# Building an expert's list of tokens: three tiles of tokens in one TensorE product in place of two

## The chip, the core and the metric

The kernel runs on one core of a Trainium2 chip. A core has a matrix engine (TensorE, PE in the profile; PEld is its weight load), VectorE (DVE), ScalarE (ACT), GpSimd (POOL) and SyncE (SP), each with an instruction queue of its own, and 16 DMA engines. The metric is the device time of one execution in microseconds. Before the change it is 648.73 us, the median of three runs (648.26 to 650.05).

## The reference, cut to what matters

Sliding-window attention (batch 8, 8 heads, 576 positions, 64 per head) makes 4608 tokens of 512 values. Then a mixture of 8 experts: all (token, expert) pairs are sorted by their logits, and in that order a token goes to an expert that has room (at most 576 tokens each). Each expert applies two matrices with a ReLU between.

```python
x = attn_out.transpose(0, 2, 1, 3).reshape(B * S, H * D)
logits = x @ w_gate
order = np.argsort(-logits.flatten())
for idx in order:                       # greedy, with capacity
    tok, e = idx // E, idx % E
    if assigned[tok] >= 0 or counts[e] >= cap:
        continue
    assigned[tok] = e; counts[e] += 1
for e in range(E):
    mask = assigned == e
    out[mask] = np.maximum(x[mask] @ w1[e], 0.0) @ w2[e]
```

## The kernel before, in words

The first part, up to about 147 us, is the attention; it also writes the token rows `xs` to DRAM and keeps the gate logits of all tokens in SBUF, 36 tiles of 128 tokens (`NJ` is 36). Then `Routing` settles one expert at a time, in eight rounds `p` = 0 to 7, and `Experts` computes each expert's two layers. From here on "list p" is the list of round p. Round 0 stands alone, since no expert is known before it. The later rounds are recorded between the matrix products of the expert before.

The order of the instructions on every engine is written by a small planner (`Streams`): generators yield a planned duration (`self.busy(...)` for an engine, `self.dve(...)` for VectorE), and the planner resumes whichever is due. Each engine then runs its instructions strictly in that order, so an instruction that has to wait holds back all that stands behind it.

A round finds by search the threshold of the next full expert (lines 530 to 620), and then makes the list of its 576 tokens, in `steps`:

- Lines 655 to 672: a running count gives each chosen token its place 0 to 575 in the list. `sb` holds the place's quotient by 32 (0 to 17) and remainder (0 to 31), for each lane and tile of tokens.
- Line 683: `A` (128 lanes x 18 x 36 tiles, bf16) is 1 where the quotient equals a row number; the 36 tiles lie innermost. Line 687 (693 in round 0) makes `B` (32 x 36) in the same way from the remainder.
- Line 685 (ScalarE) writes `A` times the lane number into `R`, and line 691 (VectorE) writes `A` times the number of the tile's first token into `R`. `R` is the stationary operand: for each product 128 columns, of which the first 72 are used.
- Line 697: 18 products, each for two tiles of tokens. The stationary operand is `R` of the two tiles, the moving operand is `B` of the two, 32 x 2 columns: runs of two neighbours (4 bytes), one run every 36 elements (72 bytes). All add up in one PSUM area `il`.
- Line 701 copies `il` to `ils`. Line 706: small products with the constant `s5` add lane and tile parts and both tiles, and lay the list out as 128 x 5. Line 711 makes the integers `idx`, with which line 964 (GpSimd) gathers the tokens' rows `xg`.

In round 0 lines 691 and 693 run in two halves of 18 tiles, and the products of a half follow it. After line 706 of round 0 come 28 products that only keep TensorE running (line 475). The rows gathered are transposed at line 888 and go into the first layer (line 1127; line 1006 in the last two experts). Lines 1160 and 1168 are the second layer. Line 1095 (ScalarE) and line 1100 (VectorE) empty the first layer's sums.

Of the kernel before, what the change touches and what calls it, by code (L numbers as in the profile page):

```python
# [11 lines left out]
BF = mybir.dt.bfloat16  # L12
HF = mybir.dt.float16
I32 = mybir.dt.int32
AF = mybir.ActivationFunctionType
OP = mybir.AluOpType
# [12 lines left out]


def attention(ctx, tc, c, q, k, v, vt, gate, xs, L, choices, setup, counters):

    nc = tc.nc
# [169 lines left out]
    load_qk(0, 2, 4, nc.scalar)  # L203
    nc.sync.dma_start(wgbd, wg)
    counters()
    load_vt(0, 0, 4)
    load_vt(0, 4, NB)
# [143 lines left out]
NJ = NT // 128  # L351
# [9 lines left out]
class Routing:  # L361


    def __init__(self, ctx, tc, c, V):
        self.tc, self.nc, self.c, self.V = tc, tc.nc, c, V
        nc = tc.nc
        rt = ctx.enter_context(tc.tile_pool(name="rt", bufs=1))
        self.rt, self.ctx = rt, ctx

        def t(name, shape, dt=FT):  # L370
            x = rt.tile(shape, dt, name=name)
            setattr(self, name, x)
            return x

        for name in ("eid", "un", "m", "best"):
            t(name, [128, NJ])
        for name in ("oh", "w", "one"):
            t(name, [128, NJ, E], BF)
        t("G0", [128, NJ, ND], BF)
        t("cw", [128, E])  # L380
        t("dg", [128, ND], I32)
        t("sh", [128, NR], I32)
        t("v5", [72, 2, 4, 5], I32)
        t("lane", [128, 1])
        t("rows", [128, 1], U32)
        self.setup = self.constants(t)
        self.idx, self.eint = {}, {}

    def counters(self):
        iota = self.nc.gpsimd.iota  # L390
        iota(self.cw, pattern=[[-1, E]], base=E, channel_multiplier=0, allow_small_or_imprecise_dtypes=True)
        iota(self.dg, pattern=[[1, ND]], base=1, channel_multiplier=0)
        iota(self.sh, pattern=[[-4, NR]], base=28, channel_multiplier=0)
        iota(self.v5, pattern=[[1, 2], [2, 4], [8, 5]], base=0, channel_multiplier=-1)
        iota(self.v5[:, :, 2:4, 4], pattern=[[1, 2], [2, 2]], base=32, channel_multiplier=-1)
        iota(self.rows, pattern=[[0, 1]], base=0, channel_multiplier=1)
        iota(self.lane, pattern=[[0, 1]], base=0, channel_multiplier=1, allow_small_or_imprecise_dtypes=True)

    def constants(self, t):

        nc, jp = self.nc, self.c["jp"]
        cw, dg, lane = self.cw, self.dg, self.lane
        cw9 = t("cw9", [128, E])
        yield nc.vector.tensor_scalar(cw9, cw, -9.0, None, op0=OP.add)
        ones = t("ones", [128, 128], BF)
        yield nc.vector.memset(ones, 1.0)
        tri = t("tri", [128, 128], BF)

        yield nc.vector.tensor_scalar(tri, jp, 0.0, -1.0, op0=OP.is_le, op1=OP.mult)
        dgf = t("dgf", [128, ND])  # L410
        yield nc.vector.tensor_copy(dgf, dg)
        tab = t("tab", [128, NR, ND], I32)
        yield nc.vector.tensor_tensor(tab, dg[:, None, :].to_broadcast([128, NR, ND]),
                                      self.sh[:, :, None].to_broadcast([128, NR, ND]), OP.logical_shift_left)
        yield nc.vector.tensor_scalar(tab[:, 0, 0:7], tab[:, 0, 0:7], -1, None, op0=OP.bitwise_xor)
        yield nc.vector.tensor_scalar(tab[:, 0, 7:15], tab[:, 0, 7:15], -2 ** 31, None, op0=OP.bitwise_xor)

        for name, n in (("r32", 32), ("r18", 18)):
            yield nc.gpsimd.iota(t(name, [128, n, NJ], BF), pattern=[[1, n], [0, NJ]], base=0, channel_multiplier=0,
                                 allow_small_or_imprecise_dtypes=True)  # L420
        yield nc.gpsimd.iota(t("row", [128, 1, NJ], BF), pattern=[[0, 1], [128, NJ]], base=0, channel_multiplier=0,
                             allow_small_or_imprecise_dtypes=True)

        diag = t("diag", [128, 4])
        gt = t("gt", [32, 5])
        yield nc.vector.tensor_scalar(gt, jp[0:32, 0:33:8], 0.0, None, op0=OP.is_le)
        for q in range(4):
            yield nc.vector.tensor_tensor(diag[32 * q:32 * q + 32], gt[:, 0:4], gt[:, 1:5], OP.subtract)
        self.sq = [t(f"sq{i}", [128, 32]) for i in range(2)]
        self.pq = [t(f"pq{i}", [128, 32]) for i in range(2)]  # L430
        for x in self.sq + self.pq:
            yield nc.vector.memset(x, 0.0)

        s5 = t("s5", [72, 2, 4, 5], BF)
        w5 = t("w5", [72, 2, 4, 5])
        yield nc.vector.tensor_scalar(w5, self.v5, 0.0, None, op0=OP.is_equal)
        yield nc.vector.scalar_tensor_tensor(s5, self.v5, -36.0, w5, op0=OP.is_equal, op1=OP.add)

        t("st", [128, 5, E])
        self.left = self.st[:, 4]  # L440
        yield nc.vector.memset(self.left, -float(CAP))
        yield nc.vector.memset(t("all8", [128, E]), 1.0)
# [39 lines left out]
    def start(self):  # L482
        self.wk = self.ctx.enter_context(self.tc.tile_pool(name="rw", bufs=2))

        self.R = self.wk.tile([128, NJ // 2, 128], BF, name="R", bufs=1)
        self.nc.scalar.activation(self.R[:, :, 72:], self.r32[:, 0:28].rearrange("p a j -> p (a j)")
                                  .rearrange("p (q w) -> p q w", w=56), AF.Copy, scale=0.0)
        self.ps = self.ctx.enter_context(self.tc.tile_pool(name="rp", bufs=1, space=PSUM))

    def dve(self, dt):  # L490
# [3 lines left out]
    def steps(self, p):  # L494

        nc, wk, V = self.nc, self.wk, self.V
        m, best, one = self.m, self.best, self.one
        slack = SLACK[p]
        tile_ = wk.tile
        X = tile_([128, 2, NJ], BF, name="X")  # L500
        code = tile_([128, 1], FT, name="code")
        if p < E - 1:
# [17 lines left out]
            base = tile_([128, 1], I32, name="base")  # L520
            rest = []
            for r in range(NR):
# [14 lines left out]
                else:  # L537
# [9 lines left out]
                    for j in range(0, NJ, 4):  # L547
                        w = one4[:, j // 4] if own else one[:, j:j + 4]
                        nc.tensor.matmul(c4, w.rearrange("p k e -> p (k e)"),
                                         G[:, j:j + 4].rearrange("p j d -> p (j d)"),  # L550
                                         start=(j == 0), stop=(j == NJ - 4))
# [44 lines left out]
                else:  # L596
# [9 lines left out]
                    if r + 1 < NR:  # L606
                        nc.vector.scalar_tensor_tensor(thr2, self.tab[:, r + 1], d[:, 0:1],
                                                       base[:, 0:1].to_broadcast([128, ND]),
                                                       op0=OP.bitwise_xor, op1=OP.bitwise_xor)
                    base = b2  # L610
# [20 lines left out]
            q = tile_([128, NJ], FT, name="q", bufs=1)  # L631
# [13 lines left out]
        else:  # L645
# [19 lines left out]
                                       op0=OP.add, op1=OP.mult)  # L665
# [8 lines left out]
        B_ = tile_([128, 32, NJ], BF, name="B", bufs=1)  # L674
        R_ = self.R
        A_ = tile_([128, 18, NJ], BF, name="A", bufs=1)
        il = self.room(128, 64)
        Rw = R_[:, :, 0:72].rearrange("p q (k a h) -> p k a q h", k=2, h=2)

        def pairs(x):  # L680
            return x.rearrange("p a (q h) -> p a q h", h=2)

        nc.vector.tensor_tensor(A_, self.r18, sb[:, 0, None, :].to_broadcast([128, 18, NJ]), OP.is_equal)
        yield self.dve(410)
        nc.scalar.activation(Rw[:, 0], pairs(A_), AF.Copy, scale=self.lane)
        if p:
            nc.vector.tensor_tensor(B_, self.r32, sb[:, 1, None, :].to_broadcast([128, 32, NJ]), OP.is_equal)
            yield self.dve(670)
        for j0, j1 in ((0, NJ),) if p else ((0, 18), (18, 36)):
            n = j1 - j0  # L690
            nc.vector.tensor_tensor(Rw[:, 1, :, j0 // 2:j1 // 2], pairs(A_[:, :, j0:j1]), pairs(self.row[:, :, j0:j1].to_broadcast([128, 18, n])), OP.mult)
            if not p:
                nc.vector.tensor_tensor(B_[:, :, j0:j1], self.r32[:, :, j0:j1],
                                        sb[:, 1, None, j0:j1].to_broadcast([128, 32, n]), OP.is_equal)
            yield self.dve(600) + slack + (500 if p else 0)
            for j in range(j0, j1, 2):
                nc.tensor.matmul(il, R_[:, j // 2], B_[:, :, j:j + 2], start=(j == 0), stop=(j == NJ - 2))
            yield self.busy(n * 29)
        yield self.dve(200) + slack
        ils = tile_([72, 32, 2], BF, name="ils")  # L700
        nc.vector.tensor_copy(ils.rearrange("p a h -> p (a h)"), il[0:72])
        yield self.dve(300)
        ip = self.room(128, 5, not p)
        for g in range(4):
            for h in range(2):
                nc.tensor.matmul(ip[32 * g:32 * g + 32], ils[:, :, h], self.s5[:, h, g], start=(h == 0), stop=(h == 1))
        if p == 0:
            self.warm(28)
        yield self.busy(100) + 200 + slack
# [4 lines left out]
        if p < E - 1:  # L714
            if not p:
# [12 lines left out]
                                           op0=OP.is_gt, op1=OP.mult)  # L728
# [573 lines left out]
```

## Time and profile before

| | |
|---|---|
| median of three runs | 648.73 us |
| profiled execution | 649.96 us, span 648.3 us |
| TensorE busy | 610.8 us (94%) |
| VectorE busy | 472.0 us (73%) |
| ScalarE busy | 342.5 us (53%) |
| GpSimd busy | 223.3 us (34%) |

The span is the time from the first to the last instruction in the trace; the rest of the execution lies around it. Busy times of different engines overlap. A matmul's duration in the trace holds the time until its result is written, so products in a row start closer to each other than one lasts: the distance is read from a row that sums up several (last end less one duration, over the number less one).

### The profile page before, as it was taken

How to read it: one execution, taken by the hardware profiler on the slowest of the kernel's cores; microseconds unless marked ns; L12 is line 12 of the kernel's file. 1: busy time of each engine (PE TensorE's matmuls, PEld its weight loads, DVE VectorE, ACT ScalarE, POOL GpSimd, SP SyncE). 2: the span in 40 equal slices, each digit the busy share in tenths (PEclk: the TensorE clock that was granted, in tenths of full speed). 3: DMA queues.
4: the chain of work that ended last, by engine and by line, in shares of the span. 5: the costliest groups of instructions: out<-in, count | busy, mean ns of one | idle time of the engine just before them, and what ended most of it. 6: DMA issues, size and time to landing. Idle time of an engine off the chain costs nothing. (4 is left out here: it accounts for less than half of the span.)

```text
span 648.3 us, 17083 instructions
## 1 busy us (share of the span) xinstructions
PE 610.8 (94%) x6423; PEld 527.8 (81%) x6423; DVE 472.0 (73%) x2127; ACT 342.5 (53%) x598; POOL 223.3 (34%) x235
## 2 busy tenths in 40 slices
PE   7899999995599999999999999999999999899995
PEld 6787887784489779978987998898789879778984
DVE  6887887787787768876877786888678875674610
ACT  2477676671255177255546537264544557766710
POOL 5455655450241062133306115131521515223211
PEclk9999999996599999999999999999999999999998
DMA  8997968991476197679659579867938638977721
GB/s 320 373 383 268 351 232 341 365 343 53 148 220 131 38 312 192 124 259 220 150 164 254 154 145 289 190 144 242 198 132 197 206 102 219 266 174 185 156 58 40
DMA packets 40338, 135.16 MB, mean 208 GB/s; under 512 B 5176, under 2 KB 5304, under 8 KB 40256
## 3 DMA queue, kind: packets, MB, share of 16 engines
q0 software_dynamic: 15568, 54.03, 36.9%
q1 hardware_dynamic: 24400, 79.52, 33.9%
q8 instruction: 51, 0.84, 0.5%
q10 hardware_dynamic: 288, 0.52, 0.3%
q14 instruction: 31, 0.25, 0.1%
HBM read 82.15 MB, written 18.87 MB: 156 GB/s over the span
## 5 line engine op out<-in xcount | busy, mean ns | idle before, releaser
L1150 POOL DMA_INDIRECT out<-ot,idx x40 | 41.6, 1041 | 195.4 <-ACT ot L1141 42.2
L1168 PE MATMUL o<-wl,hh 128*128 128x512 f32 x256 | 101.5, 396 | 2.4 <-DMA wl<-st 2.4
L1168 PE MATMUL o<-wh,hh 128*128 128x512 f32 x256 | 102.4, 400 | 0.1
L1168 PE MATMUL o<-wh,hl 128*128 128x512 f32 x256 | 101.4, 396 | 0.0
L144 POOL TENSOR_TENSOR st<-st,mx 128x512 f32<-128x512 f32 x72 | 73.4, 1039 | 66.8 <-DVE mx L137 60.6
L851 ACT ACTIVATE wh<-st 128x1024 fp32r<-128x1024 f32 x72 | 75.7, 1053 | 8.5 <-DMA st<-w 4.7
L1095 ACT ACTIVATE hh<-h 128x256 fp32r<-128x256 f32 (+1 forms) x96 | 39.0, 407 | 75.5 <-PE h L1127 74.8
L862 POOL DMA_DIRECT2D wl<-st x63 | 58.3, 1140 | 56.0 <-ACT wl L860 40.3
L964 POOL DMA_INDIRECT xg<-xs,idx x40 | 42.8, 1070 | 91.9 <-DVE eq L718 66.5
L1127 PE MATMUL h<-xh,wl 128*128 128x320 f32 (+1 forms) x384 | 70.8, 300 | 0.0
L137 DVE CUSTOM_DVE_ANT_0 st<-Sp,mask 128x128 f32<-128x128 f32 x288 | 67.2, 283 | 4.8 <-PE Sp L128 4.1
L1127 PE MATMUL h<-xh,wh 128*128 128x320 f32 (+1 forms) x384 | 69.5, 300 | 0.7 <-ACT xh L954 0.7
L1127 PE MATMUL h<-xl,wh 128*128 128x320 f32 (+1 forms) x384 | 69.6, 299 | 0.3 <-DVE xl L958 0.3
L860 ACT ACTIVATE wl<-wh 128x1024 fp32r<-128x1024 f32 x63 | 66.5, 1056 | 0.7
L1168 PEld LDWEIGHTS o<-wl,hh 128*128 128x128 f32 x256 | 48.1, 188 | 12.1 <-DMA wl<-st 3.2
L1127 PEld LDWEIGHTS h<-xh,wh 128*128 128x128 f32 x384 | 56.8, 189 | 1.4 <-ACT xh L954 0.8
L1127 PEld LDWEIGHTS h<-xh,wl 128*128 128x128 f32 x384 | 57.2, 189 | 0.3
L1127 PEld LDWEIGHTS h<-xl,wh 128*128 128x128 f32 x384 | 56.8, 189 | 0.5 <-DVE xl L958 0.5
L1168 PEld LDWEIGHTS o<-wh,hh 128*128 128x128 f32 x256 | 48.2, 188 | 9.8 <-DVE ot L1148 0.5
L1168 PEld LDWEIGHTS o<-wh,hl 128*128 128x128 f32 x256 | 48.1, 188 | 9.3
L1141 ACT ACTIVATE ot<-o 128x512 f32<-128x512 f32 x32 | 19.1, 596 | 65.9 <-PE o L1168 58.8
L152 ACT ACTIVATE pt<-Tp 128x512 f32<-128x512 f32 x72 | 39.8, 594 | 21.0 <-PE Tp L150 19.8
(227 smaller groups left out, 1282.0 us busy)
## 6 DMA issues: line engine op xcount, KB each, us to landing
wl<-st POOLq DMA_DIRECT2D x63, 512.0 KB
st<-w SPq DMA_DIRECT2D x60, 512.0 KB
V<-v SPq DMA_DIRECT2D x16, 584.0 KB
xs<-x SPq DMA_DIRECT2D x36, 256.0 KB
VT<-vt SPq DMA_DIRECT2D x8, 640.0 KB
VT<-vt SPq DMA_DIRECT2D x8, 512.0 KB
Q<-q SPq DMA_DIRECT2D x6, 640.0 KB
K<-k SPq DMA_DIRECT2D x6, 640.0 KB
```

What stands on the lines that cost most here:

```text
L137: nc.vector.tensor_tensor_reduce(st[:, h, :], Sp[h % 2][:, h // 2], mk, scale=-0.125, scalar=3.0e38, op0=OP.add, op1=OP.min, accum_out=mx[ ...
L144: nc.gpsimd.tensor_tensor(st, st, mx[:, :, None].to_broadcast([128, 4, 128]), OP.subtract)
L152: nc.scalar.activation(pt, Tp, AF.Exp, scale=-1.0)
L851: nc.scalar.activation(hi, x, AF.Copy)
L860: nc.scalar.activation(lo, hi.bitcast(FT), AF.Copy, scale=-1.0)
L862: nc.gpsimd.dma_start(lo.bitcast(FT), x, accum_op=OP.add)
L964: nc.gpsimd.indirect_dma_start(out=g[0:n, a], out_offset=None, in_=self.xs, in_offset=IndirectOffsetOnAxis(ap=idx[0:n, a:a + 1], axis=0))
L1095: nc.scalar.activation(hh[:, f, c0:c1], h, AF.Relu)
L1127: nc.tensor.matmul(h, wv[:, cc, 128 * (f % 2):128 * (f % 2) + 128], xt[:, cc, c0:c1], start=(k == 0), stop=(k == 11))
L1141: nc.scalar.activation(ot, o, AF.Copy)
L1150: nc.gpsimd.indirect_dma_start(out=self.out, out_offset=IndirectOffsetOnAxis(ap=idx[0:m, a:a + 1], axis=0), in_=ot[0:m], in_offset=None)
L1168: nc.tensor.matmul(o, ht[:, f, 128 * a:128 * a + 128], wt[:, 512 * (f % 2):512 * (f % 2) + 512], start=(f == 0 and k == 0), stop=(f == NF ...
```

## The change

Three tiles of tokens go into one product: 12 products a list with 96 moving columns each, where 18 with 64 were. In `R` 108 of the 128 columns are used, and the rows of one tile lie next to each other (18 columns for each of the three tiles, for the lane part, and then the same for the tile part); before, the two tiles alternated. Lines 685 and 691 so write runs of 54 neighbours and read `A` across its 36 tiles, one element every 72 bytes. `s5` is built for three tiles, and line 706 becomes 12 products. The planned duration of the list's products falls from 29 to 20 ns for each tile.

```diff
-        t("v5", [72, 2, 4, 5], I32)
+        t("v5", [108, 3, 4, 5], I32)
...
-        iota(self.v5, pattern=[[1, 2], [2, 4], [8, 5]], base=0, channel_multiplier=-1)
-        iota(self.v5[:, :, 2:4, 4], pattern=[[1, 2], [2, 2]], base=32, channel_multiplier=-1)
+        iota(self.v5, pattern=[[18, 3], [1, 4], [4, 5]], base=0, channel_multiplier=-1)
+        iota(self.v5[:, :, 2:4, 4], pattern=[[18, 3], [1, 2]], base=16, channel_multiplier=-1)
...
-        s5 = t("s5", [72, 2, 4, 5], BF)
-        w5 = t("w5", [72, 2, 4, 5])
+        s5 = t("s5", [108, 3, 4, 5], BF)
+        w5 = t("w5", [108, 3, 4, 5])
...
-        self.R = self.wk.tile([128, NJ // 2, 128], BF, name="R", bufs=1)
-        self.nc.scalar.activation(self.R[:, :, 72:], self.r32[:, 0:28].rearrange("p a j -> p (a j)")
-                                  .rearrange("p (q w) -> p q w", w=56), AF.Copy, scale=0.0)
+        self.R = self.wk.tile([128, NJ // 3, 128], BF, name="R", bufs=1)
+        self.nc.scalar.activation(self.R[:, :, 108:], self.r32.rearrange("p a j -> p (a j)")[:, 0:20 * NJ // 3]
+                                  .rearrange("p (q w) -> p q w", w=20), AF.Copy, scale=0.0)
...
-        il = self.room(128, 64)
-        Rw = R_[:, :, 0:72].rearrange("p q (k a h) -> p k a q h", k=2, h=2)
-        def pairs(x):
-            return x.rearrange("p a (q h) -> p a q h", h=2)
+        il = self.room(128, 96)
+        Rw = R_[:, :, 0:108].rearrange("p q (k h a) -> p k q h a", k=2, h=3)
+        def threes(x):
+            return x.rearrange("p a (q h) -> p q h a", h=3)
...
-        nc.scalar.activation(Rw[:, 0], pairs(A_), AF.Copy, scale=self.lane)
+        nc.scalar.activation(Rw[:, 0], threes(A_), AF.Copy, scale=self.lane)
...
-            nc.vector.tensor_tensor(Rw[:, 1, :, j0 // 2:j1 // 2], pairs(A_[:, :, j0:j1]), pairs(self.row[:, :, j0:j1].to_broadcast([128, 18, n])), OP.mult)
+            nc.vector.tensor_tensor(Rw[:, 1, j0 // 3:j1 // 3], threes(A_[:, :, j0:j1]), threes(self.row[:, :, j0:j1].to_broadcast([128, 18, n])), OP.mult)
...
-            for j in range(j0, j1, 2):
-                nc.tensor.matmul(il, R_[:, j // 2], B_[:, :, j:j + 2], start=(j == 0), stop=(j == NJ - 2))
-            yield self.busy(n * 29)
+            for j in range(j0, j1, 3):
+                nc.tensor.matmul(il, R_[:, j // 3], B_[:, :, j:j + 3], start=(j == 0), stop=(j == NJ - 3))
+            yield self.busy(n * 20)
...
-        ils = tile_([72, 32, 2], BF, name="ils")
-        nc.vector.tensor_copy(ils.rearrange("p a h -> p (a h)"), il[0:72])
+        ils = tile_([108, 32, 3], BF, name="ils")
+        nc.vector.tensor_copy(ils.rearrange("p a h -> p (a h)"), il[0:108])
...
-            for h in range(2):
-                nc.tensor.matmul(ip[32 * g:32 * g + 32], ils[:, :, h], self.s5[:, h, g], start=(h == 0), stop=(h == 1))
+            for h in range(3):
+                nc.tensor.matmul(ip[32 * g:32 * g + 32], ils[:, :, h], self.s5[:, h, g], start=(h == 0), stop=(h == 2))
```

Although a planned duration changes, the order of the instructions stays almost as it was. On VectorE, GpSimd and SyncE nothing moves; on ScalarE one weight copy moves past one neighbour in the last expert; on TensorE two products move. The next two pieces are VectorE at list 6, before and after. Line 691 stands between the instructions of line 1100, and line 683, which it reads, stands two places ahead.

```order
L683 TENSOR_TENSOR A<-r_466,sb 128x648
L687 TENSOR_TENSOR B<-r_394,sb 128x1152
L1100 SCALAR_TENSOR_TENSOR hl<-h,hh 128x256
L691 TENSOR_TENSOR R<-A,row 128x18x18x2
L1100 SCALAR_TENSOR_TENSOR hl<-h,hh 128x256
L1100 SCALAR_TENSOR_TENSOR hh<-h,hh 128x64
L701 CAST ils<-rps 72x64
```

After the change, at the same place (the columns at the end are the pattern of what is written):

```order
L683 TENSOR_TENSOR A<-r_466,sb 128x648
L687 TENSOR_TENSOR B<-r_394,sb 128x1152
L1100 SCALAR_TENSOR_TENSOR hl<-h,hh 128x256
L691 TENSOR_TENSOR R<-A,row 128x12x54
L1100 SCALAR_TENSOR_TENSOR hl<-h,hh 128x256
L1100 SCALAR_TENSOR_TENSOR hh<-h,hh 128x64
L701 CAST ils<-rps 108x96
```

Nothing moved; line 691 writes 12 runs of 54 in place of 18 x 18 runs of 2, and line 701 copies 96 columns. The one place where TensorE's order differs is behind list 7, before and after: line 888 transposes the last rows of expert 7, and line 706 follows.

```order
L1168 MATMUL o<-wh,hh 128x512
L1168 MATMUL o<-wl,hh 128x512
L888 MATMUL tp<-identr,xg 128x64 x4
L1168 MATMUL o<-wh,hl 128x512
L706 LDWEIGHTS ils
L706 MATMUL rps<-s_808,ils 32x5
```

After the change:

```order
L1168 MATMUL o<-wh,hl 128x512
L1168 MATMUL o<-wh,hh 128x512
L888 MATMUL tp<-identr,xg 128x64 x4
L1168 MATMUL o<-wl,hh 128x512
L706 LDWEIGHTS ils
L706 MATMUL rps<-s_808,ils 32x5
```

The transposes and line 706 stand behind two more products of the second layer than before.

## Rows read from the trace of the kernel before

**Rows 1.** Stretches: busy us of each engine, granted clock, DMA share, GB/s.

```profile
200.00:540.00 340.00, 339.61 (x2470) 296.86 (x2469) 260.87 (x1040) 174.55 (x272) 103.66 (x105) 1.00 0.70 183
170.00:173.00 3.00, 1.10 (x18) 1.07 (x18) 2.25 (x8) 0.86 (x1) 0.00 (x0) 0.50 0.72 203
```

**Rows 2.** Groups of instructions: busy us, mean ns of one, idle before.

```profile
L549 PE MATMUL rps<-G,one 128*128 128x60 bf16 x360 | 17.1, 191 | 0.0
L697 PE MATMUL rps<-B,R 128*128 128x64 bf16 x144 | 9.9, 239 | 2.7 <-ACT R L685 2.5 <-DVE R L691 0.2
L685 ACT ACTIVATE R<-A,lane 128x648 bf16<-128x648 bf16 x8 | 7.1, 887 | 27.9 <-DVE A L683 27.9
L691 DVE TENSOR_TENSOR R<-A,row 128x648 bf16<-128x648 bf16 x7 | 5.2, 740 | 0.0
L731 DVE TENSOR_REDUCE c<-oh 128x8 bf16<-128x288 bf16 x7 | 4.7, 669 | 0.2
L458 DVE TENSOR_REDUCE best<-w 128x36 f32<-128x288 bf16 x6 | 2.7, 451 | 0.2
L1168 PE MATMUL o<-wl,hh 128*128 128x512 f32 x256 | 101.5, 396 | 2.4 <-DMA wl<-st 2.4
```

**Rows 3.** Timeline, one search product group: start us, length us, engine, line.

```profile
239.58 0.43 PE L549 MATMUL rps<-G,one 128*128 128x60 bf16 x9
```

**Rows 4.** Timeline of lists 1 to 7: line 691 and the products behind.

```profile
227.19 0.73 DVE L691 TENSOR_TENSOR R<-A,row 128x648 bf16<-128x648 bf16 x1
228.37 1.24 PE L697 MATMUL rps<-B,R 128*128 128x64 bf16 x18
...
281.11 0.73 DVE L691 TENSOR_TENSOR R<-A,row 128x648 bf16<-128x648 bf16 x1
282.52 1.24 PE L697 MATMUL rps<-B,R 128*128 128x64 bf16 x18
...
337.31 0.75 DVE L691 TENSOR_TENSOR R<-A,row 128x648 bf16<-128x648 bf16 x1
338.36 1.24 PE L697 MATMUL rps<-B,R 128*128 128x64 bf16 x18
...
391.44 0.75 DVE L691 TENSOR_TENSOR R<-A,row 128x648 bf16<-128x648 bf16 x1
392.36 1.24 PE L697 MATMUL rps<-B,R 128*128 128x64 bf16 x18
...
447.64 0.73 DVE L691 TENSOR_TENSOR R<-A,row 128x648 bf16<-128x648 bf16 x1
448.51 1.24 PE L697 MATMUL rps<-B,R 128*128 128x64 bf16 x18 [0.23 <-DVE R L691]
...
502.69 0.74 DVE L691 TENSOR_TENSOR R<-A,row 128x648 bf16<-128x648 bf16 x1
503.58 1.24 PE L697 MATMUL rps<-B,R 128*128 128x64 bf16 x18
...
522.98 0.75 DVE L691 TENSOR_TENSOR R<-A,row 128x648 bf16<-128x648 bf16 x1
524.26 1.24 PE L697 MATMUL rps<-B,R 128*128 128x64 bf16 x18
```

**Rows 5.** Timeline of list 0 and of the transposes that read its rows.

```profile
170.99 0.44 DVE L691 TENSOR_TENSOR R<-A,row 128x324 bf16<-128x324 bf16 x1
171.90 0.45 DVE L693 TENSOR_TENSOR B<-r,sb 128x576 bf16<-128x576 bf16 x1
171.90 1.24 PE L697 MATMUL rps<-B,R 128*128 128x64 bf16 x18 [2.52 <-ACT R L685]
...
179.36 0.40 PEld L888 LDWEIGHTS tp<-identr,xg 128*128 128x128 f32 x4 [0.79 <-DMA xg<-xs,idx]
```

**Rows 6.** Timeline, line 706 of list 1 and the next product.

```profile
230.29 0.23 PE L706 MATMUL rps<-s,ils 72*32 72x5 bf16 x8
230.45 0.50 PE L1168 MATMUL o<-wl,hh 128*128 128x512 f32 x1
```

More of the change, by code (lines that the diff above doesn't have):

```diff
@@ L432, in constants @@
             yield nc.vector.memset(x, 0.0)
-        s5 = t("s5", [72, 2, 4, 5], BF)
-        w5 = t("w5", [72, 2, 4, 5])
+        s5 = t("s5", [108, 3, 4, 5], BF)
+        w5 = t("w5", [108, 3, 4, 5])
         yield nc.vector.tensor_scalar(w5, self.v5, 0.0, None, op0=OP.is_equal)
-        yield nc.vector.scalar_tensor_tensor(s5, self.v5, -36.0, w5, op0=OP.is_equal, op1=OP.add)
+        yield nc.vector.scalar_tensor_tensor(s5, self.v5, -54.0, w5, op0=OP.is_equal, op1=OP.add)
         t("st", [128, 5, E])
```

## The prediction, made before the result was known

> **What bounds the kernel now.** I read the stretches first, by stage; then the groups of the lines that the change touches; then the timeline around each list. In the stretches the reader is to see that TensorE is busy 339.61 of the 340 us from 200 to 540 us, at a granted clock of 1.00, the upper level of 2.4 GHz [rows 1]. All of lists 1 to 7 lie there. A microsecond of TensorE's work that goes in this stretch, or a microsecond that TensorE has to wait, so moves the end by the same amount. List 0 stands by itself: in 170 to 173 us TensorE is busy 1.10 of 3 us at a granted clock of 0.50, the lower level of 1.2 GHz, and VectorE 2.25 [rows 1]. There the chain VectorE, list, gather, transposes sets the time: the transposes at 179.36 us wait for the DMA of the gathered rows [rows 5].
>
> The groups show what the list's instructions cost [rows 2], and the timeline shows how little time lies between the end of line 691 and the first product that needs it [rows 4]. At list 5 the products already wait for line 691: it ends at 447.64 + 0.73 = 448.37 us and they start at 448.51, so the hand-over takes 0.14 us. For each list the room is the products' start, less the end of line 691, less 0.14:
>
> - list 1: 228.37 - 227.92 - 0.14 = 0.31
> - list 2: 282.52 - 281.84 - 0.14 = 0.54
> - list 3: 338.36 - 338.06 - 0.14 = 0.16
> - list 4: 392.36 - 392.19 - 0.14 = 0.03
> - list 5: 0
> - list 6: 503.58 - 503.43 - 0.14 = 0.01
> - list 7: 524.26 - 523.73 - 0.14 = 0.39
>
> **The list's products.** Eighteen products end 1.24 us after the first starts, and one lasts 0.239 [rows 2, 4]: (1.24 - 0.24) / 17 = 0.0588 us from one to the next. The search's products, with as wide a stationary operand and 60 columns that lie side by side, follow each other after (0.43 - 0.19) / 8 = 0.030 us [rows 2, 3]. So the weight load is not what holds the list's products back: it is the moving operand `B`, in runs of two every 72 bytes. How runs of three do, no row shows. From below, the pace of columns side by side would be 96 / 60 x 0.030 = 0.048; a run that costs what it costs now gives 0.0588 (32 runs, as before); a column that costs what it costs now gives 96 / 64 x 0.0588 = 0.088. I take 0.072, between the last two, because the two rows that there are leave open whether the run or the column is what is paid. Then lists 1 to 7 take 7 x 12 x 0.072 = 6.05 us where they took 7 x 18 x 0.0588 = 7.41: -1.36. The ends are 4.03 (-3.38) and 7.39 (0).
>
> **Line 706.** Eight products hold TensorE from 230.29 to 230.45 us, 20 ns each, though all eight are over 0.23 us after the first starts [rows 6]: they overlap, so from below four more cost nothing. By the row they cost 0.08 a list, which I take: +0.56 over seven lists.
>
> **Line 691, the term that decides.** Now it takes 0.740 us for 648 elements, and 0.44 for 324 in list 0 [rows 2, 5]: 0.93 ns an element and a fixed 0.14. The change makes what it writes one run of 54 and what it reads one element every 72 bytes. The nearest row of a stepped bf16 read on VectorE is line 731, 288 elements in steps of 16 bytes: 669 ns. Line 458 reads as many side by side in 451 [rows 2]. Without the fixed part that is (0.669 - 0.14) / 288 = 1.84 ns an element stepped, and 1.08 side by side. So the new line 691 takes 0.14 + 648 x 1.84 = 1.33 us, 0.59 more. From below: 0.14 + 648 x 1.08 = 0.84, 0.10 more, if the step costs nothing. From above: if the step is paid twice (1.84 + 0.76), 1.82, 1.08 more. I take 1.33, the row that reads the same type in steps.
>
> The Trainium skill weighs in here: by VectorE: DVE Perf Modes, "What auto-detection actually checks", two bf16 values are taken in one cycle only if every tensor is 16-bit with a step of one. By that rule the pairs layout qualified and the new one doesn't; an estimate from the page's clock of 0.96 GHz is 648 / 0.96 = 675 ns plus the fixed part, which is the lower end above, and the rule alone would make the line 0.10 us longer. The trace's 0.93 ns an element now is above the half cycle that the rule by itself gives, so runs of two have a price of their own here.
>
> What waits: TensorE stands still at the list's first product, and everything on it stands behind. With 0.59 us more and the room above: 0.28 + 0.05 + 0.43 + 0.56 + 0.59 + 0.58 + 0.20 = +2.69 us. On VectorE line 1100 is next behind line 691; it empties sums of the first layer, and lines 1160 and 1168 need these later, so 0.6 us there costs nothing. If that cover is gone, it is at most another 0.6 us at lists 5 and 6.
>
> **Line 685 on ScalarE.** 887 ns now, written in runs of two; then it writes runs of 54 and reads in steps. Its own row is the nearest: no change. From above, VectorE's 0.76 ns an element would be 0.49 us. It ends ahead of line 691 in lists 1 to 7, but in lists 5 and 6 line 1095 stands behind it on ScalarE, and line 1100, which reads what line 1095 writes, stands just ahead of line 691 on VectorE. So up to 2 x 0.49 could come on top; I count 0.
>
> **List 0.** Line 691 in two halves: 0.14 + 324 x 1.84 = 0.74 each, 0.30 more, so the last part of `B` ends at 172.35 + 0.60 = 172.95 us [rows 5]. Six products follow from 173.09, at 1.2 GHz: 64 columns take 53 ns of the 58.8, so 96 take 80 + 5.5 = 85 ns, and the last starts at 173.52. Before, it started at 171.90 + 17 x 0.0588 = 172.90: 0.62 later. With 32 more columns to copy at line 701 (0.03, at 1.08 ns) and four more products at line 706 (0.08) it is +0.73, all of it in front of the gather.
>
> **At nothing:** the zeroing of `R`'s unused columns (line 486), smaller than before, on a ScalarE that then waits until list 0; the constants `v5`, `s5`, built under the attention, 20 elements more each; line 701's 0.03 in lists 1 to 7, since three other products stand between the list and line 706; the two products moved past transposes at list 7, which are work in either order.
>
> **Sum:** -1.36 + 0.56 + 2.69 + 0.73 = +2.62 us. The profiled execution's 649.96 us (span 648.3) becomes 652.6. It lies 1.23 above the median of 648.73, so against the median I forecast 651.3.
>
> **Rivals.** All are told against the median.
>
> *A run of three costs what a run of two costs.* Then the lists take 7 x 12 x 0.0588 = 4.94, -2.47, and the sum is +1.51: 650.2. For it: at 1.2 and at 2.4 GHz the distance is the same (1.24 us for 18 in both [rows 4, 5]), so at the upper clock something other than columns is paid. Against it: a run of 6 bytes does not begin on a whole pair of elements in every second product. The Trainium skill, SBUF — State Buffer, "Door 1: The DMA port swizzle", says that SBUF has lines of 16 bytes, that two hits in a line hide its latency, and that a new line costs extra. By that rule a price goes with the line touched, so a run of three inside a line is no dearer; but the rule also has runs of two free, and the trace's 58.8 against 30 ns differs from it.
>
> *The column is paid, not the run.* No gain in the products: +3.98, 652.7. For it: the same rows, since two columns in a run can't tell the two apart.
>
> *Not slower: the stepped read is free.* The place is line 691, and the point from which it decides is a duration under about 0.95 us. At 0.84 TensorE waits 0.07 + 0.10 + 0.09 us at lists 4 to 6, list 0 comes 0.23 later (its halves 0.05 longer each, worked out as above), and with the products at 0.072 the sum is -1.36 + 0.56 + 0.26 + 0.23 = -0.31: 648.4. With the products at 0.0588 it is -1.42, and with columns at the full pace -2.33: 646.4. For it: line 691 already pays for short runs in what it writes, and these go. Against it: line 731 against line 458.
>
> *The step is paid twice.* Line 691 at 1.82: 0.77 + 0.54 + 0.92 + 1.05 + 1.08 + 1.07 + 0.69 = 6.12 of waiting, some 1.2 at list 0, +6.5: 655.2.
>
> *The loss is taken up later.* Near 576 us a second-layer product waits 2.4 us for weights, the one such place [rows 2]. A late TensorE could wait less there. Against it: in ScalarE's order that weight's copy stands behind an evacuation that TensorE's own transposes feed, so it moves along. Then 2.4 of the 2.62 would go and 648.9 be left.
>
> **How the numbers follow.** A measurement of this kernel tells 0.3% (1.95 us, so 646.8 to 650.7) from no change. The forecast with its own range of 650.7 to 652.2 has 0.40; the run's price 0.21 (same); the column's 0.13 (slower); the free step 0.13, about half of it faster; the step paid twice 0.05; taken up later 0.08 (same, at times faster). Slower: 0.40 + 0.13 + 0.05 = 0.58, and 0.02 of the run's price, which lies not far from the bound: 0.60. Faster: 0.08. Same: 0.32. The range of 648.3 to 653.4 leaves out the step paid twice and the faster half of the free step.
>
> **What would show it.** In the profile after: line 691 near 1.33 us for 648 elements; TensorE's idle time ahead of line 697 near 2.7 us over lists 1 to 7 with line 691 as its releaser, and the most of it at lists 4 to 6; 12 products in about 0.072 x 11 + 0.25 = 1.04 us; the transposes of list 0 some 0.7 us later. I am wrong if line 691 stays under 0.95 us, if the 12 products end within 0.8 us, or if TensorE is idle elsewhere by more than 1 us.

## The result and the profile after

The changed kernel took 654.32 us (median of 12 runs, 650.94 to 657.13). The kernel before, run alongside on the same chip, took 650.58 (12 runs, 647.79 to 654.07). The ratio is 1.0051 with an interval of 1.0029 to 1.0073: slower by about 3.3 us, where +2.62 was forecast. A second set gave 1.0069 (1.0040 to 1.0097). The time of 654.32 lies above the range that was given, 648.3 to 653.4: the loss was larger than forecast, and the kernel before itself took 1.85 us more here than in the three runs on which the forecast stood. As a ratio the forecast is 1.0040, which lies inside the first interval and at the lower end of the second; so the total alone doesn't show what was wrong, and the places below do.

Single executions differ by some us; the attention's last product (line 173) starts anywhere from 145.5 to 150.5 us. So places below are counted from the first product of the first layer (181.64 us before, 181.62 after). The first product of list 7 came 342.62 us behind it before and 347.57 after, +4.95; the last product 459.22 and 462.21, +2.99. In a second execution of each kernel (e10, e7) these are 342.78 and 347.54, and 458.50 and 463.49: list 7 repeats to 0.2 us, the end does not.

The stretch of [rows 1] in the changed kernel, and three short stretches behind list 5 (columns as there):

```profile
200.00:540.00 340.00, 335.68 (x2426) 292.24 (x2425) 263.54 (x1036) 174.36 (x266) 101.24 (x103) 0.99 0.70 181
452.00:453.00 1.00, 1.00 (x16) 0.62 (x15) 0.27 (x3) 0.97 (x2) 0.00 (x0) 0.84 0.99 397
453.00:456.00 3.00, 3.00 (x8) 2.32 (x8) 2.83 (x9) 0.14 (x1) 2.16 (x3) 0.50 0.58 210
456.00:458.00 2.00, 2.00 (x9) 1.62 (x9) 1.41 (x4) 0.95 (x2) 1.70 (x2) 0.98 0.65 164
```

TensorE is busy 335.68 us of 340, where it was busy 339.61 [rows 1], and for some 3 us it runs at a granted clock of 0.50, the lower level of 1.2 GHz. The groups that answer to [rows 2]:

```profile
L697 PE MATMUL rps<-B,R 128*128 128x96 bf16 x96 | 8.4, 239 | 6.8 <-ACT R L685 3.1 <-DVE R L691 2.7 <-ACT wh L851 0.7
L685 ACT ACTIVATE R<-A,lane 128x648 bf16<-128x648 bf16 x8 | 12.0, 1496 | 28.5 <-DVE A L683 28.5
L691 DVE TENSOR_TENSOR R<-A,row 128x648 bf16<-128x648 bf16 x7 | 9.4, 1343 | 0.0
L683 DVE TENSOR_TENSOR A<-r,sb 128x648 bf16<-128x648 bf16 x8 | 3.9, 493 | 0.2
L1168 PE MATMUL o<-wl,hh 128*128 128x512 f32 x256 | 101.8, 397 | 0.4 <-DMA wl<-st 0.4
```

Line 691 went from 740 to 1343 ns, as forecast. Line 685, which was counted as unchanged, went from 887 to 1496.

TensorE's timeline at lists 1, 3 and 5, the last products ahead of the list and the list's own:

```profile
228.27 0.39 PE L1168 MATMUL o<-wh,hl 128*128 128x512 f32 x1
228.50 0.39 PE L1168 MATMUL o<-wh,hh 128*128 128x512 f32 x1
229.04 1.02 PE L697 MATMUL rps<-B,R 128*128 128x96 bf16 x12
229.87 0.47 PE L1168 MATMUL o<-wl,hh 128*128 128x512 f32 x1
...
338.49 0.39 PE L1168 MATMUL o<-wh,hl 128*128 128x512 f32 x1
339.15 1.02 PE L697 MATMUL rps<-B,R 128*128 128x96 bf16 x12 [0.28 <-ACT wh L851]
...
448.88 0.40 PE L1160 MATMUL o<-wl,hh 128*128 128x512 f32 x1
450.74 1.02 PE L697 MATMUL rps<-B,R 128*128 128x96 bf16 x12 [1.47 <-DVE R L691]
```

A wait in brackets is counted from the modelled end of the product before. Products of 512 columns start 0.23 us apart but last 0.39, so 0.16 of each wait is not in the bracket, and list 1, which shows none, waits 229.04 - 228.50 - 0.23 = 0.31 us. Taken from start to start, less the same distance in the kernel before, the seven lists wait longer by 0.31, 0.09, 0.43, 0.58, 1.24, 1.23 and 0.22 us, together 4.10. The forecast was 0.28, 0.05, 0.43, 0.56, 0.59, 0.58, 0.20, together 2.69. The releaser named at list 3, line 851, is only what ended about then; line 691 had ended 0.15 us ahead.

What made lists 5 and 6 double, from ScalarE's and VectorE's timeline at list 5:

```profile
447.11 1.50 ACT L685 ACTIVATE R<-A,lane 128x648 bf16<-128x648 bf16 x1 [1.02 <-DVE A L683]
448.51 0.37 ACT L1095 ACTIVATE hh<-h 128x256 fp32r<-128x256 f32 x1
448.92 0.42 DVE L1100 SCALAR_TENSOR_TENSOR hl<-h,hh 128x256 fp32r<-128x256 f32 x1 [1.17 <-ACT hh L1095]
449.26 1.34 DVE L691 TENSOR_TENSOR R<-A,row 128x648 bf16<-128x648 bf16 x1
```

Line 1095 stands behind line 685 on ScalarE, line 1100 waits 1.17 us for it, and line 691 stands behind line 1100 on VectorE. So the 0.61 us of line 685 and the 0.60 of line 691 both go into TensorE's wait. The same chain stands in the kernel before, where line 1100 already waited 0.54 us for it:

```profile
446.12 0.89 ACT L685 ACTIVATE R<-A,lane 128x648 bf16<-128x648 bf16 x1 [1.02 <-DVE A L683]
446.90 0.36 ACT L1095 ACTIVATE hh<-h 128x256 fp32r<-128x256 f32 x1
447.30 0.42 DVE L1100 SCALAR_TENSOR_TENSOR hl<-h,hh 128x256 fp32r<-128x256 f32 x1 [0.54 <-ACT hh L1095]
```

List 0, first two rows of the kernel before that belong to [rows 5], then the changed kernel:

```profile
170.46 0.49 DVE L683 TENSOR_TENSOR A<-r,sb 128x648 bf16<-128x648 bf16 x1
173.76 0.17 DVE L711 CAST idx<-h 128x5 uint32<-128x5 f32 x1 [0.36 <-PE h L706]
```

```profile
170.30 0.50 DVE L683 TENSOR_TENSOR A<-r,sb 128x648 bf16<-128x648 bf16 x1
...
172.38 1.29 PE L697 MATMUL rps<-B,R 128*128 128x96 bf16 x12 [3.15 <-ACT R L685]
...
174.38 0.17 DVE L711 CAST idx<-h 128x5 uint32<-128x5 f32 x1 [0.41 <-PE h L706]
...
179.24 0.39 PEld L888 LDWEIGHTS tp<-identr,xg 128*128 128x128 f32 x4 [0.64 <-DMA xg<-xs,idx]
```

From line 683 to `idx` it takes 174.38 - 170.30 = 4.08 us where it took 173.76 - 170.46 = 3.30, so the list is ready 0.78 us later, but the transposes begin 8.94 us behind line 683 (before 8.90).

### The profile page after: what moved, and what is told of

It is laid out like the page before. It is cut to its first block, busy times and chain, and to the rows that moved or that the text cites. A ratio compares the mean times of both kernels' runs of the same rounds, so it can differ in the third digit from the quotient of the medians.

```text
span 651.3 us, 17051 instructions
## 1 busy us (share of the span) xinstructions
PE 610.5 (94%) x6407; PEld 526.4 (81%) x6407; DVE 477.0 (73%) x2127; ACT 346.2 (53%) x598; POOL 224.1 (34%) x235
```

## The experiments

Ratios are against the kernel before, run alongside on the same chip. The edits are cut to the lines that matter; the constants that go with them (`v5`, `u5`, `r18`, `row`) are left out.

**e1: the stationary order alone.** The pairs of the kernel before, with `R` in runs of 18 rows for each of the two tiles.

```
-        Rw = R_[:, :, 0:72].rearrange("p q (k a h) -> p k a q h", k=2, h=2)
+        Rw = R_[:, :, 0:72].rearrange("p q (k h a) -> p k q h a", k=2, h=2)
-            return x.rearrange("p a (q h) -> p a q h", h=2)
+            return x.rearrange("p a (q h) -> p q h a", h=2)
```

> The kernel before with one part of the change alone: pairs of tiles and 18 products as before, but R in runs of 18 rows for each tile, so that lines 685 and 691 read A in steps. Theory A (the stepped reads of lines 691 and 685 hold TensorE back): line 691 1.34 us and line 685 1.50 us for 648 elements, TensorE idle ahead of the list's products by 3 us or more over lists 1 to 7, most at lists 5 and 6; ratio to before 1.004 to 1.009, slower than the change itself by the 1.2 us that the twelve products save. Rival B (products of three tiles, or line 706 with twelve, are dearer): none of them is here, so ratio 0.999 to 1.001. Rival C (the loss is a matter of the order of instructions and of chance in the tail): ratio 0.998 to 1.002 with the waits at the lists present or not.

Measured: 1.0092 (1.0062 to 1.0123). The lines were as slow as in the changed kernel:

```profile
L685 ACT ACTIVATE R<-A,lane 128x648 bf16<-128x648 bf16 x8 | 12.0, 1496 | 27.9 <-DVE A L683 27.9
L691 DVE TENSOR_TENSOR R<-A,row 128x648 bf16<-128x648 bf16 x7 | 9.4, 1343 | 0.0
```

The waits were 0.26, 0.42, 1.46 and 1.22 us in brackets at lists 3 to 6, and the clock fell behind both list 5 and list 6 (0.97 in 450 to 500 us, 0.96 in 500 to 540). All of the loss is there without products of three; without their gain, and with a second fall of the clock, the kernel is slower than the changed one.

**e2: three tiles, the columns alternating.** The changed kernel with `R`'s rows in the order of the kernel before.

```
-        Rw = R_[:, :, 0:108].rearrange("p q (k h a) -> p k q h a", k=2, h=3)
+        Rw = R_[:, :, 0:108].rearrange("p q (k a h) -> p k a q h", k=2, h=3)
-            return x.rearrange("p a (q h) -> p q h a", h=3)
+            return x.rearrange("p a (q h) -> p a q h", h=3)
```

> The changed kernel with the columns of R alternating between the three tiles, as the pairs did: lines 685 and 691 read A along its tiles and write runs of three; 12 products and line 706 with twelve stay. Theory A: line 691 0.74 to 0.86 us, line 685 0.87 to 0.95, products at 0.0705 us from one to the next, TensorE idle at lists 1 to 7 under 0.6 us in all, no fall of the granted clock in 200 to 540 us; the time is before less 7 x (0.21 - 0.04) = 1.2 us, ratio 0.997 to 0.999. Rival B: ratio 1.002 to 1.005, as the change. Rival C: ratio 1.000 to 1.005, unlike its waits.

Measured: 1.0034 (1.0015 to 1.0053), so the loss did not go. The expectation missed the cost of a run of three in what is written:

```profile
L685 ACT ACTIVATE R<-A,lane 128x648 bf16<-128x648 bf16 x8 | 11.1, 1388 | 28.5 <-DVE A L683 28.5
L691 DVE TENSOR_TENSOR R<-A,row 128x648 bf16<-128x648 bf16 x7 | 8.8, 1260 | 0.0
```

The waits in brackets were 0.18, 0.35, 1.18 and 0.94 us at lists 3 to 6; the clock stayed at 1.00.

**e3: the products planned later.** The changed kernel, with 1.4 us more planned ahead of the products of lists 1 to 7.

```
-            yield self.dve(600) + slack + (500 if p else 0)
+            yield self.dve(600) + slack + (1900 if p else 0)
```

> The changed kernel with 1400 ns more planned between line 691 and the list's products in rounds 1 to 7, so that they stand some six second-layer products later in TensorE's order; every instruction stays as long as in the changed kernel. Theory A (waiting, not the work, is what costs): lines 691 and 685 1.34 and 1.50 us as in the changed kernel, but TensorE idle at lists 1 to 7 under 0.3 us in all and the granted clock at 1.00 from 200 to 540 us; ratio to before 0.997 to 1.000. Rival B: as the change, 1.003 to 1.007. Rival D (VectorE's and ScalarE's longer instructions hold back the first layer's sums and cost there): ratio 1.002 to 1.005 with waits at lines 1127, 1160 or 1168 of 1 us or more.

Measured: 1.0208 (1.0175 to 1.0240). The waits at the lists went, as expected, but the ratio missed, since the rounds end later and other products wait. TensorE's waits from 200 us on:

```profile
PE h L1006 <- ACT xh L904: 4.2, 1, 4.2
PE rps L549 <- DVE G L468: 3.2, 1, 3.2
PE tp L888 <- DVE t L913: 2.3, 1, 2.3
PE rps L706 <- DVE ils L701: 1.7, 1, 1.7
```

The clock was 0.69 in 540 to 560 us, and it also fell at the search's wait of 3.2 us:

```profile
258.00:262.00 4.00, 3.19 (x21) 3.19 (x22) 3.64 (x17) 2.37 (x4) 4.00 (x5) 0.58 0.76 173
```

So asking for the lists 1.4 us later moves the waits to other places of the rounds and makes them longer.

**e4: `A` by tile.** The changed kernel, with `A` turned so that both lines read and write neighbours (`row` is spread to the same shape); the lines are 684, 686 and 692 there.

```
-        A_ = tile_([128, 18, NJ], BF, name="A", bufs=1)
+        A_ = tile_([128, NJ, 18], BF, name="A", bufs=1)
-        nc.vector.tensor_tensor(A_, self.r18, sb[:, 0, None, :].to_broadcast([128, 18, NJ]), OP.is_equal)
+        nc.vector.tensor_tensor(A_, self.r18, sb[:, 0, :, None].to_broadcast([128, NJ, 18]), OP.is_equal)
```

> The changed kernel with A made tile by tile (36 x 18, the 18 rows innermost) and the tiles' first tokens spread to the same shape beforehand, so that lines 685 and 691 read and write neighbours. Theory A: line 685 0.74 us, line 691 0.48 (two values a cycle) to 0.84, line 683 0.82 in place of 0.49, because the place is then spread over the innermost rows; the three together end at most 0.1 us later than before, TensorE idle at lists 1 to 7 under 0.6 us, ratio 0.996 to 1.000. Rival B: ratio 1.003 to 1.006.

Measured: 0.9993 (0.9970 to 1.0017). The line that makes `A` went from 0.493 to 0.830 us, and the two others became the fastest seen:

```profile
L686 ACT ACTIVATE R<-A,lane 128x648 bf16<-128x648 bf16 x8 | 6.7, 836 | 30.9 <-DVE A L684 30.8
L692 DVE TENSOR_TENSOR R<-A,row 128x648 bf16<-128x648 bf16 x7 | 3.4, 487 | 0.0
```

The only wait shown at a list is 0.30 us at list 5. So with neighbours the loss is gone. A gain does not show in the ratio; in the profiled execution TensorE waited 0.9 us for the search (line 549 before) between 260 and 270 us, which the other executions shown, e3 apart, did not.

**e5: ScalarE's line slow again.** From e4, the lane half of `R` alternates, so that ScalarE reads `A` 36 bytes apart (line 689; VectorE's is 695).

```
-        nc.scalar.activation(Rw[:, 0], threes(A_), AF.Copy, scale=self.lane)
+        nc.scalar.activation(R_[:, :, 0:54].rearrange("p q (a h) -> p q a h", h=3), A_.rearrange("p (q h) a -> p q a h", h=3), AF.Copy, scale=self.lane)
```

> From the variant with A by tile (e4), ScalarE's line alone is made slow again: it reads A 36 bytes apart (rows of A, three tiles side by side in R's lane half); VectorE's line keeps neighbours on both sides. Theory A (both lines lie one behind the other before the products of lists 5 and 6, VectorE's alone before those of lists 1 to 4 and 7): ScalarE's line goes from 0.84 to about 1.4 to 1.5 us, VectorE's stays at 0.49, TensorE's wait grows by about 0.6 us at lists 5 and 6 alone (list 5 from 0.30 to about 0.9, list 6 from nothing to 0.3 to 0.6), the other lists stay without a wait, the clock stays at 1.00, and the time is 0 to 1 us (0 to 0.15%) above that variant: ratio 0.999 to 1.002. Rival B (the prediction as it counted: ScalarE's line is hidden at every list): the waits stay as in e4. Rival C (36 bytes apart read as fast as neighbours): the line stays near 0.84.

Measured: 0.9999 (0.9978 to 1.0020). The line took 996 ns, not 1.4 to 1.5 us, so the run tells little of the wait: it grew by the same 0.16 us at list 5 (0.46) and to 0.22 at list 6.

```profile
L689 ACT ACTIVATE R<-A,lane 128x648 bf16<-128x648 bf16 x8 | 8.0, 996 | 30.9 <-DVE A L687 30.9
L695 DVE TENSOR_TENSOR R<-A,row 128x648 bf16<-128x648 bf16 x7 | 3.4, 491 | 0.8 <-ACT R L689 0.8
```

The second row shows a side effect of this edit, and of those of e6 and e9: VectorE's line now waits for ScalarE's, which it does not in e4.

**e6: VectorE's line slow again.** From e4, the tile half alternates, read 36 bytes apart (line 700; `mixed` turns `A` and `row` alike).

```
+        Rt = R_[:, :, 54:108].rearrange("p q (a h) -> p q a h", h=3)
+            nc.vector.tensor_tensor(Rt[:, j0 // 3:j1 // 3], mixed(A_[:, j0:j1]), mixed(self.row[:, j0:j1]), OP.mult)
```

> From the variant with A by tile (e4), VectorE's line alone is made slow again: it reads A and the row table 36 bytes apart; ScalarE's line keeps neighbours. Theory A: VectorE's line goes from 0.49 to about 1.3 us, ScalarE's stays at 0.84; every list's products are asked for 0.8 us later, and TensorE waits 0.2 to 0.5 us at lists 3 and 4, about 1.1 at list 5 and 0.3 to 0.9 at list 6; these sum to 2 to 3 us, of which part is taken up later; ratio 1.001 to 1.005 against the kernel before, and 0.001 to 0.004 above e4. Rival B (the waits of the changed kernel come mostly from ScalarE's line): waits under 0.3 us at lists 5 and 6. Rival D (its waits are those of the planned order, not of this line): waits as in e4.

Measured: 1.0034 (1.0011 to 1.0057). The line took 856 ns, not 1.3 us, and the waits in brackets were 0.22 at list 1, 0.18 at list 4, 0.66 at list 5 and 0.41 at list 6: 0.36 more at list 5 than in e4, for a line 0.37 longer. List 1's wait is the side effect told at e5, 0.23 us ahead of line 700.

**e7: the changed kernel once more.**

> The changed kernel once more, unaltered, for the one thing a single profile can't tell: whether TensorE's clock falls after list 5's wait of 1.5 us by rule or by chance, and whether the wait for wl near 576 us is again short. Theory A (the wait itself brings the fall): granted clock about 0.97 in the window of 50 us that holds list 5, with line 1160's products about 0.43 us apart for some 3 us behind the wait. Rival (chance of that execution): clock 1.00 there, with the same wait of 1.4 to 1.5 us. Lines 685 and 691 at 1.50 and 1.34 us in either. Ratio 1.003 to 1.008.

Measured: 1.0069 (1.0040 to 1.0097). The waits came back to 0.02 us (0.26, 0.42, 1.48, 1.23), and the clock fell in the same place:

```profile
453.00:456.00 3.00, 3.00 (x20) 2.31 (x20) 2.38 (x9) 0.82 (x1) 1.78 (x2) 0.60 0.54 180
456.00:458.00 2.00, 2.00 (x8) 1.57 (x7) 1.74 (x5) 0.26 (x1) 1.39 (x3) 0.74 0.65 213
```

The wait for `wl` was 1.7 us, not 0.4.

**e8: the wait filled.** The changed kernel with 24 products of 96 columns ahead of lists 5 and 6, whose result is overwritten.

```
+            for _ in range(24 if p in (5, 6) else 0):
+                nc.tensor.matmul(il, self.ones, self.r32.rearrange("p a j -> p (a j)")[:, 0:96], start=True, stop=True)
             for j in range(j0, j1, 3):
```

> The changed kernel, and ahead of the products of lists 5 and 6 stand 24 products of 96 columns each whose result is overwritten, so that TensorE works through about 1 us of the waits of 1.47 and 1.22 us. Theory A (the clock falls since TensorE stands still there): the granted clock stays at 1.00 behind both lists, line 1160's products stay 0.23 us apart, the lists' products still start when line 691 ends, and some 1.6 us of the loss go wherever the changed kernel's clock fell: ratio 0.997 to 1.000 against the changed kernel in the same call, 1.002 to 1.005 against the kernel before. Rival (the fall has another cause, as the run of slow columns itself): clock 0.97 in the same window and no gain. Should the fillers run past the end of line 691, the lists' products start up to 0.4 us later.

Measured: 1.0051 (1.0033 to 1.0068). Behind list 5 the clock no longer falls:

```profile
453.00:456.00 3.00, 3.00 (x14) 2.43 (x14) 2.86 (x8) 0.65 (x2) 2.32 (x3) 1.00 0.40 135
```

The products of list 5 start in the same place (269.08 us, changed kernel 269.12 and 269.10), those of list 6 at 325.18 instead of 326.80 and 326.77. So the fall costs 1.6 us, and it is gone where TensorE works through the wait. The mean granted clock of whole executions agrees: 0.977 in the 12 of e8, 0.975 in the 8 of e7. In the medians the 1.6 us can't be told: 654.05 against 654.73.

**e9: ScalarE's line alone, slower still.** As e5, but written as runs of three, one to each stationary tile in turn.

```
-        nc.scalar.activation(R_[:, :, 0:54].rearrange("p q (a h) -> p q a h", h=3), A_.rearrange("p (q h) a -> p q a h", h=3), AF.Copy, scale=self.lane)
+        nc.scalar.activation(R_[:, :, 0:54].rearrange("p q (a h) -> p a q h", h=3), A_.rearrange("p (q h) a -> p a q h", h=3), AF.Copy, scale=self.lane)
```

> ScalarE's line once more slow alone, since e5's form cost it only 0.996 us: it reads A by tile 36 and 108 bytes apart and writes runs of three bf16, one to each of the stationary tiles in turn, as in e2 (1.388 there); VectorE's two lines as in e4 (0.83 and 0.487). From the runs so far: TensorE's wait at list 5 is the sum of line A, ScalarE's line and VectorE's line less some 1.88 us (before 2.12 and 0.23, e4 2.15 and 0.30, e5 2.31 and 0.46, e6 2.52 and 0.66, e2 3.14 and 1.18, changed 3.34 and 1.47), that at list 6 some 0.25 less. Theory A (ScalarE's line stands whole in the chain of lists 5 and 6, and nowhere else): with the line at 1.3 to 1.5 us the wait is 0.75 to 1.0 at list 5 and 0.5 to 0.75 at list 6, and lists 1 to 4 and 7 go without a wait; ratio 1.000 to 1.003. Rival (ScalarE's line hidden, as the prediction counted it; e2's and the changed kernel's waits follow VectorE's line with a factor): waits as in e4, 0.30 and 0.

Measured: 1.0065 (1.0045 to 1.0086), above what was expected.

```profile
L689 ACT ACTIVATE R<-A,lane 128x648 bf16<-128x648 bf16 x8 | 12.4, 1547 | 30.9 <-DVE A L687 30.9
L695 DVE TENSOR_TENSOR R<-A,row 128x648 bf16<-128x648 bf16 x7 | 3.5, 494 | 2.8 <-ACT R L689 2.8
```

```profile
451.18 1.52 ACT L689 ACTIVATE R<-A,lane 128x648 bf16<-128x648 bf16 x1 [1.36 <-DVE A L687]
453.01 0.42 DVE L1104 SCALAR_TENSOR_TENSOR hl<-h,hh 128x256 fp32r<-128x256 f32 x1 [1.19 <-ACT hh L1099]
453.35 0.48 DVE L695 TENSOR_TENSOR R<-A,row 128x648 bf16<-128x648 bf16 x1
453.98 1.02 PE L701 MATMUL rps<-B,R 128*128 128x96 bf16 x12 [0.99 <-ACT wh L855]
```

With VectorE's line at 494 ns the wait is 0.99 us at list 5 and 0.75 at list 6, as expected: line 695 starts there when line 1104 ends (1100 before), which waited 1.19 us for line 1099 (1095 before), which stood behind line 689. At lists 1, 2 and 4 it waits 0.59, 0.37 and 0.40, which was not expected: that is the side effect told at e5 (0.39 us ahead of line 695 at list 3), and it does not exist in the changed kernel, where line 691 starts while line 685 still runs. List 0 is later too, 5.07 us from line 687 to `idx` where e4 takes 3.61.

At list 5 seven kernels now stand side by side: the three lines that make `A` and the two halves of `R`, added up, and TensorE's wait in brackets.

| kernel | A + lane + tile, us | wait, us | more than before: lines, wait |
|---|---|---|---|
| before | 0.49 + 0.89 + 0.74 = 2.12 | 0.23 | |
| e4 | 0.83 + 0.84 + 0.49 = 2.15 | 0.30 | 0.03, 0.07 |
| e5 | 0.83 + 1.00 + 0.49 = 2.32 | 0.46 | 0.20, 0.23 |
| e6 | 0.83 + 0.84 + 0.86 = 2.52 | 0.66 | 0.40, 0.43 |
| e9 | 0.83 + 1.55 + 0.49 = 2.87 | 0.99 | 0.75, 0.76 |
| e2 | 0.49 + 1.39 + 1.26 = 3.14 | 1.18 | 1.02, 0.95 |
| changed | 0.49 + 1.50 + 1.34 = 3.33 | 1.47 | 1.21, 1.24 |

What is added to ScalarE's line or to VectorE's goes into the wait whole, to within 0.07 us.

**e10: the kernel before once more.**

> The kernel before once more, unaltered, for its profile: how far its landmarks and its wait for wl near 576 us (2.4 us in the profiled execution shown, 0.4 to 1.7 in the other kernels) repeat. If the wait for wl stands where it was by rule (the changed kernel gives part of its loss back there): 2 us or more again, and the end 459 us behind the first product of the first layer. If it varies by chance: anything from 0.4 to 2.4, with the lists' waits (0.23 at list 5, none elsewhere) and their places within 0.2 us of the first profile.

Measured: 650.66 us, one run. List 7's products at 342.78 (342.62), the last product at 458.50 (459.22), and the one wait at a list again 0.23. TensorE's wait for `wl`:

```profile
PE o L1168 <- DMA wl<-st: 2.0, 3, 0.8
```

This wait is 2.4 and 2.0 us in the kernel before, 0.4 and 1.7 in the changed one, 2.2 in e1, 1.2 in e8 and e9, 1.4 in e2, e4 and e6, and 0.4 in e5. It may give some of the loss back, but two executions of one kernel differ as much as the two kernels.

## Why the prediction was right or wrong

*What it is about* held: TensorE bounds the stretch, its waits at the lists move what stands behind them, and line 691 makes them at lists 1 to 4 and 7. Line 691 was forecast at 1.33 us and took 1.343; at lists 1 to 4 and 7 the longer waits were forecast at 1.52 us together and came to 1.63. e1 and e4 show that the order in which `A` is read, and not the products of three, brings the loss. That line 691's size came out so close is luck in part: it was taken from a reduction that reads in steps of 16 bytes, and in e6 the same line, reading 36 bytes apart, took only 0.856 us.

*The step that failed* is the one on line 685: "Its own row is the nearest: no change", with an upper bound of 0.49 us. It measured +0.61. The mechanism by which that would count was named there (line 1095 behind it, line 1100 behind that), but the term was sized at nothing. Lists 5 and 6 each waited 0.65 us longer than forecast, and 0.61 of that is this line; e9, with ScalarE's line slow alone, shows it going into the wait whole. The row of the line itself was no guide, since it tells nothing of a stepped read; and rows of the kernel before showed that the line was not hidden: line 1100 waited 0.54 us behind it at list 5, and [rows 5] name it as what list 0's first product waited for.

*What was not in the sum* is the clock: behind list 5's wait it fell, and that cost 1.6 us (e7, e8). The stretch of [rows 1] at 0.50, where TensorE was busy 1.10 of 3 us, had shown that the clock is low where TensorE stands still, but no step of the sum asked what a longer wait does to the clock.

*The list's products* came 0.0705 us apart on the mean, (1.02 - 0.245) / 11, against 0.072. The value was set between two rivals, and that it came out is luck, for the trace shows two kinds of product. In list 2 the twelve start 55, 77, 84, 65, 60, 80, 81, 68, 59, 77 and 86 ns apart, within 4 ns the same in lists 1 to 7, while products of runs of two start 59 to 61 ns apart from the third on. The dear ones are products 2, 3, 6, 7, 10 and 11. A run of three begins 6 bytes further with each product and 72 with each row, so (if `B` begins on a multiple of 16 bytes) half the runs of just these six lie across such a multiple; no other run does. A run that lies across costs more, one that doesn't costs nearly what a run of two costs. From the first of them to the next product's start it is 0.83 us where it was 1.05, so they give 7 x 0.22 = 1.54 (forecast 1.36).

*Line 706* costs less than its term: from its start to the next product's start it is 230.93 - 230.74 = 0.19 us in list 1, and 0.19 or 0.20 in lists 2 to 6, where it was 0.15 or 0.16, so about +0.3 over seven lists where +0.56 stood.

*List 0's* +0.73 came at the list itself (+0.78 at `idx`), but what it is worth can't be told. From `idx` to the first transpose it took 4.89 and 5.00 us in the changed kernel and 5.63 and 6.01 in the kernel before; but it took 5.02 in e8 and 5.94 in e3, whose list 0 is that of the changed kernel. So the time until the gathered rows are there varies by more than the term, and why was not tried.

*The two rules weighed.* By the Trainium skill, VectorE: DVE Perf Modes, "What auto-detection actually checks", two bf16 values go in one cycle if every tensor is 16-bit with a step of one; an estimate for line 691 without that, from the page's 0.96 GHz, is 0.675 + 0.14 = 0.82 us, 0.08 more than before. The measured 0.60 more differs, so most of it is something else than the lost pairing. With neighbours on every tensor (e4) the line takes (0.487 - 0.14) / 648 = 0.54 ns an element, which agrees with two values in a cycle of the page's 0.96 GHz. By the Trainium skill, SBUF — State Buffer, "Door 1: The DMA port swizzle", SBUF has lines of 16 bytes, and an access that crosses to a new line costs extra. The trace agrees as to the products of three: those whose runs stay inside such a line come 55 to 68 ns apart, those of which half the runs lie across two 76 to 86. So the first rival's price (a run of three costs nearly what a run of two costs) held for half of the products.

*The loss taken up later* stays open, as told at e10.

By the measured terms the sum is -1.54 + 0.3 + 4.10 + 1.6 = +4.5 us, with list 0 left out, of which up to 2 may return at the wait for `wl`; the two ratios say +3.3 and +4.5. The forecast's direction and its main term were right, its size was short by the two terms above. That the total came no further off is in part luck: 1.3 us were missing at lists 5 and 6 and 1.6 for the clock, while line 706 and the products stood 0.4 too high and what list 0's 0.73 is worth can't be told.

No variant is measurably faster than the kernel before. e4 keeps the 12 products without the waits and stands at 0.9993, with 1 inside its interval.

## What to carry to other kernels

When an edit turns an access pattern, price every instruction that reads or writes the turned tile, on each engine, with a row of the new pattern; the row of the same line in its old pattern says nothing. Then follow each lengthened line through the queues: two lines on two engines add up where a third instruction links them, even if each seems hidden alone. And a wait of TensorE may cost more than itself, as the 1.47 us at list 5 did: look at the granted clock behind it, and put filler products there to tell the two apart. Where a moving operand is read in short runs, look at which runs lie across a multiple of 16 bytes before their price is taken from one mean.

## What the runs showed of the hardware that was not expected

For the same 648 bf16 elements VectorE's line took 0.487 us with neighbours read and written, 0.740 with runs of two written, 0.856 with reads 36 bytes apart, 1.260 with runs of three written and 1.343 with reads 72 bytes apart. ScalarE's took 0.836, 0.887, 0.996, 1.388 and 1.496 in the same order. So on both engines a run of three written costs far more than a run of two. The two stepped reads differ both in their distance and in how many elements follow one another so (3 with 36 bytes, 18 with 72), and no run tells which of the two matters.

TensorE's products with a moving operand in runs of three came 55 to 68 ns apart where no run lay across a multiple of 16 bytes, and 76 to 86 where half of them did; with runs of two, which never do, 59 to 61.

The clock fell to 0.50 behind a wait of 1.47 us in all three executions that had it (e1, the changed kernel twice) and at one of 3.2 us (e3), and not behind 1.18 (e2) or 0.99 (e9). Behind the same 1.22 us at list 6 it fell in e1 and not in the changed kernel, so the length of the wait alone does not decide.
